# The two normalizations of tile 17 on VectorE, moved ahead of three of its other instructions

## The chip, the core and the metric

The kernel runs on one core of a Trainium2 chip. A core has TensorE (PE, matrix multiplications into the eight banks of PSUM), VectorE (DVE), ScalarE (ACT), GpSimd (POOL) and SyncE (SP, here only an issuer of DMAs), each with its own instruction queue that runs in order. The metric is the device time of one execution, in microseconds (us); of several runs the median is given.

## What is computed

Two layers, one behind the other, for 4 sequences of 768 tokens. The first is a retention layer with 8 heads of 64 channels. In the form of a recurrence, for each batch and head with its decay gamma:

```python
state = gamma * state + outer(k[t], v[t])
y[t] = (1 / sqrt(D)) * q[t] @ state
```

The heads' y side by side are the 512 channels of x. The second layer normalizes and applies two matrices with a relu between them, and adds x:

```python
xn = (x - mean(x)) / sqrt(var(x) + 1e-6) * g_ln
out = x + relu(xn @ w_ch1) @ w_ch2          # 512 -> 2048 -> 512
```

## The kernel before

The 3072 tokens are cut into 24 tiles of 128: tiles 0 to 3 are the first of each sequence, 4 to 8 the other five of sequence 0, 9 to 13 those of sequence 1, 14 to 18 of sequence 2, 19 to 23 of sequence 3. In each tile the recurrence is written as a masked product of scores within the tile plus a product of q with the state of the tiles before.

The whole program is one long list of tokens (ORDER, lines 36 to 96). Each token calls a small function that issues a few instructions. Nothing reorders them: every engine runs its instructions in the order in which the tokens stand, and the framework adds the semaphore waits between the engines, for data, for buffers that are used again, and also where two engines read the same PSUM bank one after the other. A number behind the letters is the tile (or group), "a" and "b" are the even and the odd heads, "/A" or "/S" is an engine, and what stands behind "//" names PSUM banks. The tokens that matter here:

- k, q, v (GpSimd, L337): loads of a tile. gk, gq, gv (GpSimd, L366): one element copied out of a buffer that is to be loaded again, which makes GpSimd's queue wait until the buffer is free.
- tr (SP, L380): one DMA that transposes q and k of a tile. eq (VectorE, L386): the transposed q times a table of scales, 128x512, both inputs bf16 in SBUF.
- vg (GpSimd, L457): v times a table of decays, 128x512, both inputs in SBUF.
- pd (TensorE, L465): adds a tile's contribution to the state in bank PD. pb (VectorE, L475, two instructions): writes a scaled copy of it, the state for the next tile.
- vis (TensorE, L395 and L401): the "visit" of a pair of tiles. Scores of the first tile (8 matmuls), of the second (8), then 16 matmuls L401 of q with the state, which open banks Y0 and Y1 anew. Y0 takes the even heads of both tiles, Y1 the odd ones.
- am (VectorE, L408): scores times the mask. py (TensorE, L423): these times v, on top of Y.
- bn (VectorE, L431 and L432): mean and variance of y. xn (VectorE, L441): (y - mean) times g_ln, from bank Y to SBUF. xc (ScalarE, L447): a plain copy of y from bank Y to SBUF, for the sum at the end. sq (ScalarE, L508): the square roots of a group's variances; rs (VectorE, L513) the reciprocals.
- ex (SP, L495): the transposition of xn by DMA. m (TensorE, L520): a group's product with w_ch1, in banks X0 to X3. r (L531 on ScalarE): the relu of it, to SBUF.
- z (TensorE, L543): a tile's product with w_ch2 in four parts. ad (VectorE, L550): that times 1/deviation plus x. st (ScalarE's queue, L557): the store.

The tiles are processed in pairs from tile 8 on, and z of one tile, m and r of a group, and the visits are woven into each other, so that TensorE has work all the time. The pair of the change, 16 and 17, has its statistics behind it, and the next visit is that of tiles 18 and 19. On TensorE the order there is m10_14, z12_1, z12_2, z12_3, vis18, pd20, z13_0, z13_1, py18; on ScalarE r10_14, xc16b, sq11, xc16a, xc17a, xc17b; on GpSimd gv20, vg20, gq21, vg21, vg22, k23, v23; on SP tr21, ex17, ex16, tr22.

The three functions whose calls change places, or that stand next to them:

```python
    def _(eng, t):   # eq
        x = bank(("tp", "q", t), True) if t < T0 else slot(tr, t - T0)[:, 0:NPAIR, :]
        nc.vector.tensor_tensor(out=slot(trq, t), in0=x, in1=qsc, op=ALU.mult)
...
    def _(eng, t, half):   # xn
        dst, src, g = y_parts(t, half, slot(xns, t))
        nc.vector.scalar_tensor_tensor(out=dst, in0=src, scalar=mv[:, t, 0:1], in1=g,
                                       op0=ALU.subtract, op1=ALU.mult)
...
    def _(eng, t, half):   # xc
        dst, src, _ = y_parts(t, half, x_all[:, t, :])
        nc.scalar.copy(out=dst, in_=src)
```

Of the kernel before, what the change touches and what calls it, by code (L numbers as in the profile page):

```python
# [72 lines left out]
xc15a r10_6/A vis16//X0,X2,X3,X1 z10_3 am17a am17b m11_6//X3 ad10 gv18 v21 gv19 m11_8//X1  # L73
r11_8/A r11_6/A am16a am16b z11_0//M k21 gk20 vg19/ q21 v22 py16 m11_2//X1 r11_2/A py17 pd3
z11_1 bn16 pb19 m10_8//X1 m10_12//X2 xn16a bn17 gk21 m11_4//X3 z11_2 q22 k22 q23 r11_4/A r10_8/A
z11_3 gv20 r10_12/A m11_10//X1 vg20/ xn16b ad11 pd19 gq21 r11_10/A z12_0//M m10_14//X0 eq18 tr21
vg21/ pb20 xn17a eq19 xn17b vg22/ z12_1 r10_14/A xc16b z12_2 sq11 xc16a xc17a xc17b z12_3 k23
v23 vis18//X3,X0,X1,X2 ad12 ex17/S ex16/S tr22 pd20 am18b z13_0//M am18a z13_1 am19a py18 z13_2
bn18 z13_3 xn18b am19b m11_12//X0 py19 m11_0//X3 xn18a ad13 bn19 ex18/S m11_14//X2 st10/A
r11_0/A xn19b z14_0//M z14_1 r11_14/A xn19a eq21 st13/A xc19b r11_12/A xc18a xc18b z14_2 rs11  # L80
pb21 eq20 ex19/S sq12 xc19a z14_3 tr23 vis20//X1,X2,X0,X3 ad14 pd21 am21a z15_0//M z15_1 eq22
am20a am21b am20b z15_2 pb22 py21 py20 m12_1//X2 bn20 r12_1/A xn20b xn20a m12_4//X1 r12_4/A
# [565 lines left out]
```

## Time and profile before

| what | us |
|---|---|
| median of 3 runs | 212.17 (212.1 to 215.47) |
| the profiled execution, its own time | 212.35 |
| its span, first to last instruction | 210.5 |
| TensorE busy | 204.3 |
| VectorE busy | 127.7 |
| ScalarE busy | 76.9 |
| GpSimd busy | 96.5 |

The profile is of one execution. A row of a timeline gives the start in us from the beginning of the span, the length, the engine, the line of the kernel, the operation, the tile written and the tiles read (without their numbers, so that tile 18's rows are told from tile 19's by the written order), and the number of merged instructions; in brackets stands the idle time of the engine before it and what ended it. In the list of waits a row gives who waited for whom, the sum in us, how often, and the longest. PEld are TensorE's weight loads, which run beside its matmuls. The granted clock of TensorE was 1.000 for the whole span.

### The profile page before, as it was taken

Reading aid. Unit: us, or ns where it says so; the run is one execution under the profiler, and the core shown is the slowest. Engines: PE = TensorE matmul, PEld = TensorE weight load, DVE = VectorE, ACT = ScalarE, POOL = GpSimd, SP = SyncE. Lnnn points to the kernel's source line nnn. Section 1 sums busy time; section 2 is a strip of 40 time slices with the busy share of each in tenths; the row PEclk is TensorE's granted clock in tenths of the full one; section 3 lists DMA queues with packets and bytes.
Section 4 is the critical chain, followed back from the end, with each engine's and each line's share of the span. In section 5 each row is a group of like instructions: output and inputs, shape, how many; then the busy total and the mean of one; then the engine's idle time right before and its main releaser. Section 6 shows DMA issues by size and latency. Waiting matters only on the chain.

```text
span 210.5 us, 4985 instructions
## 1 busy us (share of the span) xinstructions
PE 204.3 (97%) x2031; PEld 131.8 (63%) x2031; DVE 127.7 (61%) x297; ACT 76.9 (37%) x168; POOL 96.5 (46%) x145
## 2 busy tenths in 40 slices
PE   7898999999999999999999999999999999999994
PEld 2467999897548667676587686475545444444443
DVE  4797889587248878578695566868948402110023
ACT  6265653642400334515237124314281522346000
POOL 8996593495597797780587449500000000000000
PEclk9999999999999999999999999999999999999999
DMA  9999999999999999999999999996032400015005
GB/s 127 172 181 180 163 195 167 125 172 161 159 121 190 123 178 138 150 118 188 225 145 172 170 166 110 137 108 149 1 104 100 101 0 3 0 50 201 0 3 199
DMA packets 109946, 27.11 MB, mean 129 GB/s; under 512 B 102625, under 2 KB 106977, under 8 KB 109922
## 3 DMA queue, kind: packets, MB, share of 16 engines
q0 software_dynamic: 77024, 13.37, 84.6%
q1 hardware_dynamic: 28242, 6.85, 24.0%
q10 hardware_dynamic: 4656, 6.56, 9.7%
q8 instruction: 16, 0.26, 0.5%
q14 instruction: 8, 0.07, 0.1%
HBM read 27.30 MB, written 6.29 MB: 160 GB/s over the span
## 4 chain that ended last, share of the span: by engine, by line
PE 89%; DVE 8%; ACT 1%; issue 1%; DVEq 0%; ACTq 0%
PE X L520 38%; PE M L543 25%; PE Y L543 9%; PE PD L543 4%; PE X L395 3%; PE Y L423 3%; PE PD L465 2%; PE PD L564 2%; DVE trq L386 2%; DVE asb L408 2%; DVE xn L441 1%; PE Y L401 1%; DVE mask L303 1%; PE Y L372 1%; DVE bns L431 1%
## 5 line engine op out<-in xcount | busy, mean ns | idle before, releaser
L520 PE MATMUL X<-xnt,w 128*128 128x128 bf16 (+2 forms) x896 | 93.9, 257 | 0.0
L531 ACT ACTIVATE h<-X 128x512 bf16<-128x512 f32 x89 | 51.2, 602 | 80.6 <-PE X L520 68.7
L520 PEld LDWEIGHTS <-w 128*128 128x128 bf16 x896 | 66.1, 98 | 20.5 <-issue 0.2
L543 PE MATMUL M<-w,h 128*128 128x512 bf16 x256 | 61.5, 379 | 0.0
L543 PEld LDWEIGHTS <-h 128*128 128x128 bf16 x400 | 37.3, 98 | 37.9
L408 DVE TENSOR_TENSOR asb<-X,mask 128x512 bf16<-128x512 f32 x48 | 30.6, 684 | 11.1 <-PE X L395 10.8
L457 POOL TENSOR_TENSOR vg<-v,vsc 128x512 bf16<-128x512 bf16 x20 | 21.3, 1069 | 9.7 <-DMA v<-in_v_dram 8.6
L550 DVE SCALAR_TENSOR_TENSOR osb<-M,rstd,x_all 128x512 f32<-128x512 f32 x16 | 11.9, 746 | 20.4 <-PE M L543 20.0
L447 ACT CAST x_all<-Y 128x256 bf16<-128x256 f32 (+1 forms) x39 | 14.3, 410 | 26.4 <-DVE xn L441 26.4
L337 POOL DMA_DIRECT2D v<-in_v_dram x24 | 21.8, 910 | 3.7 <-DMA w<-in_moe_w_ch_dram 2.5
L431 DVE BATCH_NORM_STATS2 bns<-Y 128x6 f32<-128x256 f32 (+1 forms) x39 | 16.3, 455 | 9.2 <-PE Y L423 9.0
L543 PE MATMUL Y<-w,h 128*128 128x512 bf16 (+1 forms) x96 | 21.8, 370 | 0.0
L441 DVE SCALAR_TENSOR_TENSOR xn<-Y,mv,gb 128x256 bf16<-128x256 f32 (+1 forms) x39 | 18.7, 513 | 1.2 <-PE Y L423 0.6
L475 DVE TENSOR_TENSOR state<-PD,gch 64x256 bf16<-64x256 f32 x40 | 16.6, 415 | 0.6 <-PE PD L465 0.3
L337 POOL DMA_DIRECT2D qk<-in_q_dram x17 | 15.2, 895 | 1.1 <-issue 1.1
L337 POOL DMA_DIRECT2D qk<-in_k_dram x17 | 15.3, 898 | 0.9 <-issue 0.7
L550 DVE SCALAR_TENSOR_TENSOR osb<-PD,rstd,x_all 128x512 f32<-128x512 f32 (+1 forms) x3 | 1.9, 618 | 20.1 <-PE PD L543 20.1
L386 DVE TENSOR_TENSOR trq<-tr,qsc 128x512 bf16<-128x512 bf16 x17 | 10.1, 597 | 3.6 <-DMA tr<-qk 3.4
L366 POOL COPY scrap<-qk 1x1 bf16<-1x1 bf16 x28 | 5.5, 195 | 11.5 <-DMA qk<-in_k_dram 9.7
L564 PE MATMUL PD<-zeros 128*128 128x512 bf16 (+1 forms) x33 | 9.0, 410 | 1.2 <-DVE zeros L250 1.2
L423 PEld LDWEIGHTS <-asb 128*128 128x128 bf16 x192 | 8.0, 98 | 3.5 <-DVE asb L408 1.6
L543 PE MATMUL PD<-w,h 128*128 128x512 bf16 (+1 forms) x48 | 8.8, 326 | 0.0
(75 smaller groups left out, 131.8 us busy)
## 6 DMA issues: line engine op xcount, KB each, us to landing
out_dram<-osb ACTq DMA_DIRECT2D x23, 256.0 KB, 2.4
w<-in_moe_w_ch_dram POOLq DMA_DIRECT2D x8, 512.0 KB, 9.2
v<-in_v_dram POOLq DMA_DIRECT2D x24, 128.0 KB, 6.6
qk<-in_k_dram POOLq DMA_DIRECT2D x17, 128.0 KB, 6.7
qk<-in_q_dram POOLq DMA_DIRECT2D x17, 128.0 KB, 5.5
k<-in_k_dram POOLq DMA_DIRECT2D x6, 128.0 KB, 8.2
q<-in_q_dram POOLq DMA_DIRECT2D x6, 128.0 KB, 7.8
tr<-qk SPq DMA_TRANSPOSE x17, 5.5
```

The costliest lines, as they stand in the source:

```text
L337: nc.gpsimd.dma_start(out=dst, in_=tok[kind][TILES[t]])
L386: nc.vector.tensor_tensor(out=slot(trq, t), in0=x, in1=qsc, op=ALU.mult)
L408: nc.vector.tensor_tensor(out=slot(asb, t)[:, :, par, :], in0=bank(("pa", t, par)).rearrange("p (i t) -> p i t", t=P), in1=mask.rearrange( ...
L423: nc.tensor.matmul(dst, lhsT=slot(asb, t)[:, h // 2, h % 2, :], rhs=v_of(t)[:, h, :], start=(not late and n == H and h == 0), stop=(h >= H ...
L431: nc.vector.bn_stats(out=bns[:, t, i, :], in_=x)
L441: nc.vector.scalar_tensor_tensor(out=dst, in0=src, scalar=mv[:, t, 0:1], in1=g, op0=ALU.subtract, op1=ALU.mult)
L447: nc.scalar.copy(out=dst, in_=src)
L457: nc.gpsimd.tensor_tensor(out=slot(vgs, chunk(t)), in0=v_of(t), in1=vsc[:, c, :].unsqueeze(2).to_broadcast([P, H, D]), op=ALU.mult)
L475: nc.vector.tensor_tensor(out=slot(state, chunk(t) - 1)[o, :, o], in0=pd[o, :, o], in1=gch[o, c - 1, :].unsqueeze(2).to_broadcast([D, NPAI ...
L520: nc.tensor.matmul(bank(("mm", g, ho))[:, j * n * P:(j + 1) * n * P], lhsT=w1[:, ko, (ho + j) * P:(ho + j + 1) * P], rhs=x[:, x0:x0 + n, k ...
L531: nc.scalar.activation(out=dst, in_=src, func=AF.Relu)
L543: nc.tensor.matmul(bank(("m2", t, piece))[:, 0:hi - lo], lhsT=slot(h1, t // 4)[:, ho, t % 4 * P:(t % 4 + 1) * P], rhs=w2[:, ho, lo:hi], st ...
```

## The change

Two tokens, xn17a and xn17b, which stood on both sides of eq19, are moved up by some tokens, to stand ahead of eq18. They pass eq18, tr21, vg21, pb20 and eq19; of these eq18, pb20 and eq19 are VectorE's. All other tokens keep their order; most of the lines of the diff are only wrapped anew.

```diff
 z11_3 gv20 r10_12/A m11_10//X1 vg20/ xn16b ad11 pd19 gq21 r11_10/A z12_0//M m10_14//X0 eq18 tr21
-vg21/ pb20 xn17a eq19 xn17b vg22/ z12_1 r10_14/A xc16b z12_2 sq11 xc16a xc17a xc17b z12_3 k23
-v23 vis18//X3,X0,X1,X2 ad12 ex17/S ex16/S tr22 pd20 am18b z13_0//M am18a z13_1 am19a py18 z13_2
...
+z11_3 gv20 r10_12/A m11_10//X1 vg20/ xn16b ad11 pd19 gq21 r11_10/A z12_0//M m10_14//X0 xn17a
+xn17b eq18 tr21 vg21/ pb20 eq19 vg22/ z12_1 r10_14/A xc16b z12_2 sq11 xc16a xc17a xc17b z12_3
+k23 v23 vis18//X3,X0,X1,X2 ad12 ex17/S ex16/S tr22 pd20 am18b z13_0//M am18a z13_1 am19a py18
...
```

More of the change, by code (lines that the diff above doesn't have):

```diff
@@ L75 @@
 z11_1 bn16 pb19 m10_8//X1 m10_12//X2 xn16a bn17 gk21 m11_4//X3 z11_2 q22 k22 q23 r11_4/A r10_8/A
-z11_3 gv20 r10_12/A m11_10//X1 vg20/ xn16b ad11 pd19 gq21 r11_10/A z12_0//M m10_14//X0 eq18 tr21
-vg21/ pb20 xn17a eq19 xn17b vg22/ z12_1 r10_14/A xc16b z12_2 sq11 xc16a xc17a xc17b z12_3 k23
-v23 vis18//X3,X0,X1,X2 ad12 ex17/S ex16/S tr22 pd20 am18b z13_0//M am18a z13_1 am19a py18 z13_2
-bn18 z13_3 xn18b am19b m11_12//X0 py19 m11_0//X3 xn18a ad13 bn19 ex18/S m11_14//X2 st10/A
+z11_3 gv20 r10_12/A m11_10//X1 vg20/ xn16b ad11 pd19 gq21 r11_10/A z12_0//M m10_14//X0 xn17a
+xn17b eq18 tr21 vg21/ pb20 eq19 vg22/ z12_1 r10_14/A xc16b z12_2 sq11 xc16a xc17a xc17b z12_3
+k23 v23 vis18//X3,X0,X1,X2 ad12 ex17/S ex16/S tr22 pd20 am18b z13_0//M am18a z13_1 am19a py18
+z13_2 bn18 z13_3 xn18b am19b m11_12//X0 py19 m11_0//X3 xn18a ad13 bn19 ex18/S m11_14//X2 st10/A
 r11_0/A xn19b z14_0//M z14_1 r11_14/A xn19a eq21 st13/A xc19b r11_12/A xc18a xc18b z14_2 rs11
```

## The prediction

> **What bounds the kernel now.** I read the page first: the busy shares, then the chain that ended last.
>
> ```profile
> span 210.5 us, 4985 instructions
> PE 204.3 (97%) x2031; PEld 131.8 (63%) x2031; DVE 127.7 (61%) x297; ACT 76.9 (37%) x168; POOL 96.5 (46%) x145
> PE 89%; DVE 8%; ACT 1%; issue 1%; DVEq 0%; ACTq 0%
> ```
>
> TensorE is nearly always busy and makes 89% of the chain. So a change of VectorE's order can win only where TensorE stands still, and can lose only by making it stand still. The list of waits for TensorE from 30 to 160 us has one entry:
>
> ```profile
> PE Y L401 <- ACT x_all L447: 0.3, 1, 0.3
> ```
>
> Next I looked for its place, in TensorE's timeline. These are the visits 18 and 20 (start, length, line). The second is the same stretch with nothing in its way.
>
> ```profile
> 133.79 0.62 PE L395 MATMUL X<-trq,tr 64*128 64x128 bf16 x16
> 134.72 0.67 PE L401 MATMUL Y<-state,trq 64*128 64x64 bf16 x16 [0.30 <-ACT x_all L447]
> 135.31 0.40 PE L465 MATMUL PD<-vg,qk 128*128 128x128 bf16 x4
> ...
> 145.64 0.62 PE L395 MATMUL X<-trq,tr 64*128 64x128 bf16 x16
> 146.09 0.40 PE L401 MATMUL Y<-state,trq 64*128 64x64 bf16 x16
> 146.42 0.40 PE L465 MATMUL PD<-vg,qk 128*128 128x128 bf16 x4
> ```
>
> From the first score matmul to pd there are 1.52 us in visit 18 (135.31 - 133.79) and 0.78 in visit 20 (146.42 - 145.64). The wait costs 0.74 us of TensorE's time; the 0.3 of the list is a part of it, since the weight loads stall too. It is the only such place, so 0.74 us is also the most that this change can win.
>
> Who makes it? ScalarE's copies of x (xc), then VectorE's xn17b, then eq19. ScalarE's and VectorE's timelines:
>
> ```profile
> 131.31 0.60 ACT L531 ACTIVATE h<-X 128x512 bf16<-128x512 f32 x1 [1.36 <-PE X L520]
> 133.56 0.37 ACT L447 CAST x_all<-Y 128x256 bf16<-128x256 f32 x1 [1.66 <-DVE xn L441]
> ...
> 128.47 0.75 DVE L550 SCALAR_TENSOR_TENSOR osb<-M,rstd,x_all 128x512 f32<-128x512 f32 x1 [1.96 <-PE M L543]
> 129.14 0.42 DVE L386 TENSOR_TENSOR trq<-tr,qsc 128x512 bf16<-128x512 bf16 x1
> 129.57 0.86 DVE L475 TENSOR_TENSOR state<-PD,gch 64x256 bf16<-64x256 f32 x2
> 130.46 0.49 DVE L441 SCALAR_TENSOR_TENSOR xn<-Y,mv,gb 128x256 bf16<-128x256 f32 x1
> 130.86 2.27 DVE L386 TENSOR_TENSOR trq<-tr,qsc 128x512 bf16<-128x512 bf16 x1
> 133.06 0.47 DVE L441 SCALAR_TENSOR_TENSOR xn<-Y,mv,gb 128x256 bf16<-128x256 f32 x1
> ```
>
> By the written order these six are ad11, eq18, pb20, xn17a, eq19, xn17b. All four xc stand behind xn17b, which ended at 133.53, and they ran from 133.56 to 134.94; the last two matmul waits end at 134.72 and 134.99. And xn17b was late because eq19 took 2.27 us where the median of its kind is 0.42. GpSimd's timeline gives the cause I take:
>
> ```profile
> 129.69 1.03 POOL L457 TENSOR_TENSOR vg<-v,vsc 128x512 bf16<-128x512 bf16 x1
> 130.68 0.18 POOL L366 COPY scrap<-qk 1x1 bf16<-1x1 bf16 x1
> 130.81 2.03 POOL L457 TENSOR_TENSOR vg<-v,vsc 128x512 bf16<-128x512 bf16 x2
> ```
>
> These are vg20, gq21, and vg21 with vg22. eq19 came 0.05 us after vg21 began and ended 0.29 us after vg22's end (133.13 against 132.84): held, then run. The xn beside vg20 (130.46, 0.49 us) was not held.
>
> **The change, part by part.** No instruction is added or removed. VectorE's order becomes ad11, xn17a, xn17b, eq18, pb20, eq19, ad12. The other engines keep their order.
>
> *xn17a and xn17b, earlier.* Their input is long there (bn17 ends at 126.17) and an xn follows another at 0.40 us elsewhere (pairs take 0.88). xn17a starts at 129.14 in eq18's old place, xn17b ends at 129.14 + 0.88 = 130.02. That is 3.51 us earlier than 133.53.
>
> *What waits for xn17b.* ScalarE has the relu r10_14 (131.31 to 131.91) ahead of the xc, so the four xc with sq11 start at about 131.9, not at 130.0. With the same 1.38 us (133.56 to 134.94) they end at 133.3. Undisturbed, TensorE wants to begin L401 at 133.79 + 0.45 = 134.24. The wait is gone, with 0.9 us to spare. SP's two transposes ex17 and ex16 go out at about 130.1 instead of 133.59, tr22 behind them goes earlier if its loads have landed, and st10 on ScalarE's queue (133.58 before) goes some 2 us earlier. None is near an end: group 12 reads those transposes at 149.71, and eq21 and eq22, which need tr21 and tr22, stand at 143.40 and 147.01 with no idle time before them. I cost the earlier DMA traffic at nothing; that slack of over 6 us covers it.
>
> *eq18, later.* It used to end at 129.56, before vg20. Now it comes at about 129.95, inside vg20 (129.69 to 130.72). It is held; the question is until when. The nearest rows:
>
> ```profile
> 73.85 1.06 POOL L457 TENSOR_TENSOR vg<-v,vsc 128x512 bf16<-128x512 bf16 x1
> 74.84 0.40 POOL L366 COPY scrap<-qk 1x1 bf16<-1x1 bf16 x1
> 73.92 1.28 DVE L386 TENSOR_TENSOR trq<-tr,qsc 128x512 bf16<-128x512 bf16 x1
> ```
>
> There, an eq waits for one vg followed by a gate copy, just as vg20 is followed by gq21. It ended at 75.20, 0.29 us after the vg, and the copy behind was stretched from 0.18 to 0.40. So the eq gets in before the copy. That is the low end: eq18 ends at 130.72 + 0.29 = 131.0, gq21 at about 131.05. The high end comes from eq19's own row, where an eq stayed out over the end of a vg into the next: eq18 then ends at 133.13. I take the low end, since vg and then copy is exactly the order here.
>
> *pb20 and eq19.* pb20 (0.86) runs from 131.0 to 131.85; its input is there from 129.5. eq19 follows at 131.85, inside vg21, which the held copy has moved to about 131.0 to 132.05. With vg22 straight behind, eq19's old row says it waits for both: vg22 ends at 133.05, eq19 at 133.35. At the other end it gets in between and ends at 132.35. Both are before 133.79, when TensorE ends z12_3 and comes to visit 18, so the two ends cost the same: nothing. GpSimd's k23 and v23 go out about 0.25 us later, with eq23 at 151.85.
>
> In the Trainium skill, the page "SBUF — State Buffer", section "Who interferes with whom", says that a VectorE instruction with two SBUF inputs and a GpSimd instruction that reads SBUF block each other fully, the later one until the first finishes. This rule speaks against the change, which moves eq18 from ahead of vg20 to a place inside it; the trace agrees on the hold (2.27 us against 0.42) but eq19 stayed out past the instruction that was first, which the section doesn't foresee. By the section alone eq18 ends at 131.0 and eq19 at about 132.3; by the 2.27 us row for both they end at 133.1 and 134.4; the sum is -0.74 by the one and about -0.3 by the other.
>
> *What is late next.* With pd at 134.57, z13_0 wants bank M at 134.81. ad12 frees it at 134.65 (133.90 + 0.75, it waits for z12_3 and not for the change); ScalarE's release of L401 took 0.05 us, so some 0.1 us is left. py18 moves to 136.54 and needs am18a (135.85). bn18 has 1.31 us of idle time ahead, of which 0.74 goes. Behind it TensorE is busy without a break to 207.6, so the gain stays.
>
> **Sum.** -0.74 us on TensorE's path, 0 for the rest: span 210.5 to 209.8, and that execution's own 212.35 to 211.6. The median shown is 0.18 below that execution, which would give 211.4. I predict 211.5.
>
> **Rivals.**
>
> *B: eq18 is held to the end of vg22.* For it: eq19's 2.27 us row. Against it: the row at 73.92. eq18 ends at 133.13, pb20 at 133.95, eq19 at 134.37. Visit 18 starts with tile 18 and stands before tile 19 until about 134.43; the rest (0.23 of scores, 0.33 of L401) puts pd at 134.99, where 135.31 was. Gain 0.32: 211.9.
>
> *C: slower.* One mechanism: B's hold, with GpSimd's chain of vg later against TensorE. Place: the wait of tile 19's score matmuls for eq19. It decides from eq19's end at 134.70 on, that is with vg22 ending after 133.17 instead of 132.84; every 0.1 us beyond costs 0.1. GpSimd waits for loads shortly before (2.87 us for qk, to 126.49), so a shift of 1 us is possible. eq19 then ends at 135.4, pd starts at 136.0: +0.7, or 212.9. Against it: the first hold must be long, too.
>
> *D: nothing changes,* because ScalarE's copies wait for something else or L401 does. Then 212.2. Against it: ScalarE's row names xn, and its start follows xn17b's end by 0.03 us.
>
> **How the numbers follow.** Chances: forecast 0.62, B 0.18, D 0.07, C 0.13. The forecast's own range is 211.2 to 211.8 (the offset of 0.18 to the median either way, and 0.1 for ad12). The range goes from 211.1 to 212.9, which takes in B, D and most of C. 2% is 4.2 us, about what a measurement of this kernel can tell from no change, and no case here reaches it. For a mechanism that I have not seen I leave 0.02 below and 0.05 above: one of the runs before was at 215.47, so this kernel can lose more than the parts above explain.
>
> **What would show it.** Right: both xn between 129.1 and 130.1; the xc at about 131.9; no wait at L401, and 0.78 us from the first score matmul to pd; eq18 at about 1.05 us, a gate copy of 0.4, eq19 at about 1.5. Wrong: eq18 over 2 us (B), TensorE waiting at L395 for trq (B or C), the xc still ending close to L401's start (D), or a new wait of z13_0 for ad12.

## The result, and the profile after

The changed kernel takes 211.13 us (median of 21 runs, 210.53 to 214.24), the kernel before, run beside it, 212.76 (21 runs, 211.12 to 215.47). The ratio is 0.994 with a 95% interval of 0.9913 to 0.9967: a gain of 1.27 us, somewhere between 0.70 and 1.85. The ratio compares the means without the few slow runs (211.32 and 212.59), so it says less than the 1.63 us between the medians. The 211.13 us lie within the range, 0.03 above its lower end, and the gain is small, as forecast. But the traces show that the path to it was not the one that was forecast.

The page of the changed kernel, first the span and the engines' busy time:

```profile
span 209.7 us, 4961 instructions
PE 202.2 (96%) x2007; PEld 131.6 (63%) x2031; DVE 127.7 (61%) x297; ACT 76.7 (37%) x168; POOL 95.4 (45%) x145
```

The work is the same (the few matmuls missing on TensorE are missing from the record, since its weight loads are as many as before). The span is 0.8 us shorter. The list of TensorE's waits, from 30 to 160 us, no longer holds the one entry of before; it has three others:

```profile
PE M L543 <- issue: 0.5, 3, 0.2
PE X L395 <- DVE trq L386: 0.3, 1, 0.3
PE M L543 <- DVE osb L550: 0.2, 1, 0.2
```

L401 waits for ScalarE's copies no more. In its place L395 waits for trq, which is what eq writes; the waits at L543 lie between 75 and 118 us, ahead of the change. TensorE's timeline shows where, at visit 18:

```profile
133.16 0.40 PE L395 MATMUL X<-trq,tr 64*128 64x128 bf16 x8
133.84 0.40 PE L395 MATMUL X<-trq,tr 64*128 64x128 bf16 x8 [0.28 <-DVE trq L386]
134.06 0.41 PE L401 MATMUL Y<-state,trq 64*128 64x64 bf16 x16
134.41 0.40 PE L465 MATMUL PD<-vg,qk 128*128 128x128 bf16 x4
```

The eight score matmuls of tile 18 run, those of tile 19 stand 0.28 us, and L401 follows at once. From the first score matmul to pd there are 1.25 us (134.41 - 133.16). Before it was 1.52, undisturbed it is 0.78. So the change wins 0.27 us here, and leaves 0.47. VectorE's timeline:

```profile
127.85 0.75 DVE L550 SCALAR_TENSOR_TENSOR osb<-M,rstd,x_all 128x512 f32<-128x512 f32 x1 [1.96 <-PE M L543]
128.51 0.87 DVE L441 SCALAR_TENSOR_TENSOR xn<-Y,mv,gb 128x256 bf16<-128x256 f32 x2
129.30 3.26 DVE L386 TENSOR_TENSOR trq<-tr,qsc 128x512 bf16<-128x512 bf16 x1
132.48 0.85 DVE L475 TENSOR_TENSOR state<-PD,gch 64x256 bf16<-64x256 f32 x2
133.36 0.43 DVE L386 TENSOR_TENSOR trq<-tr,qsc 128x512 bf16<-128x512 bf16 x1
```

And GpSimd's and ScalarE's:

```profile
129.11 1.03 POOL L457 TENSOR_TENSOR vg<-v,vsc 128x512 bf16<-128x512 bf16 x1
130.10 0.18 POOL L366 COPY scrap<-qk 1x1 bf16<-1x1 bf16 x1
130.24 2.03 POOL L457 TENSOR_TENSOR vg<-v,vsc 128x512 bf16<-128x512 bf16 x2
...
131.17 0.37 ACT L447 CAST x_all<-Y 128x256 bf16<-128x256 f32 x1
131.62 0.92 ACT L447 CAST x_all<-Y 128x256 bf16<-128x256 f32 x3
```

The xn pair is done at 129.38 and the copies at 132.54, well ahead of L401, as forecast. But eq18 took 3.26 us: it stood from 129.30 behind vg20, the gate copy, vg21 and vg22, and ended at 132.56, 0.29 us after the last of them (132.27). pb20 and eq19 came behind it, and eq19 ended at 133.79. TensorE wanted it at about 133.4. This is rival B.

The rest of the 0.8 us has nothing to do with visit 18: it began at 133.16 instead of 133.79, 0.63 us earlier. The shift was there ahead of the change: ad11, VectorE's last instruction before it, came at 127.85 instead of 128.47, and TensorE had started visit 8 at 61.83 instead of 62.83. So in single profiles positions ahead of the change scatter by more than it wins. Behind it nothing is given back: from pd20 to the first score matmul of visit 20 there are 10.32 us, and 10.33 before.

### The profile page after: what moved, and what is told of

Same layout as the page of the kernel before. It is cut to its first block, busy times and chain, and to the rows that moved or that the text cites. A ratio compares the mean times of both kernels' runs of the same rounds, so it can differ in the third digit from the quotient of the medians.

```text
span 209.7 us, 4961 instructions
## 1 busy us (share of the span) xinstructions
PE 202.2 (96%) x2007; PEld 131.6 (63%) x2031; DVE 127.7 (61%) x297; ACT 76.7 (37%) x168; POOL 95.4 (45%) x145
## 4 chain that ended last, share of the span: by engine, by line
PE 54%; DVE 4%; issue 1%
PE X L520 23%; PE M L543 16%; PE Y L543 6%; PE PD L543 4%; DVE trq L386 2%; PE X L395 2%; PE Y L423 1%; PE PD L465 1%; DVE state L475 1%; PE Y L401 1%; DVE osb L550 1%; DVE xn L441 0%; DVE rstd L513 0%
## 5 line engine op out<-in xcount | busy, mean ns | idle before, releaser
L543 PEld LDWEIGHTS <-h 128*128 128x128 bf16 x400 | 37.4, 98 | 38.2 <-issue 0.3
L543 PE MATMUL M<-w,h 128*128 128x512 bf16 x238 | 59.4, 379 | 1.5 <-issue 0.5
L543 PE MATMUL Y<-w,h 128*128 128x512 bf16 (+1 forms) x93 | 21.7, 370 | 0.2
L386 DVE TENSOR_TENSOR trq<-tr,qsc 128x512 bf16<-128x512 bf16 x17 | 10.8, 643 | 3.5 <-DMA tr<-qk 3.3
L564 PE MATMUL PD<-zeros 128*128 128x512 bf16 (+1 forms) x32 | 8.5, 402 | 1.2 <-DVE zeros L250 1.2
L366 POOL COPY scrap<-qk 1x1 bf16<-1x1 bf16 x28 | 4.9, 176 | 9.8 <-DMA qk<-in_k_dram 8.5
L543 PE MATMUL PD<-w,h 128*128 128x512 bf16 (+1 forms) x46 | 8.4, 324 | 0.1
```

The costliest lines, as they stand in the source:

```text
L543: nc.tensor.matmul(bank(("m2", t, piece))[:, 0:hi - lo], lhsT=slot(h1, t // 4)[:, ho, t % 4 * P:(t % 4 + 1) * P], rhs=w2[:, ho, lo:hi], st ...
```

## The experiments

A correction first. The gate copies of GpSimd were described above as waiting for a buffer to be free. In the trace they wait for a load to land, such as that of k21 for 2.87 us, to 126.49. GpSimd's timeline of the kernel before:

```profile
126.49 0.18 POOL L366 COPY scrap<-qk 1x1 bf16<-1x1 bf16 x1 [2.87 <-DMA qk<-in_k_dram]
```

The chain of vg follows from there at GpSimd's own pace: vg20 starts 3.19 to 3.28 us after this copy in all nine profiles of the table further down. This matters below.

The diffs are cut to the tokens of one engine, in that engine's order; the other engines' tokens that stand between them are left out. "Stretch" is the time on TensorE from visit 18's first score matmul to pd20: 0.78 if nothing waits. T1 and T2 differ on where the 1.27 us come from, T3 on what sets the gain, T4 and T5 on when a held eq gets in.

### e1 and e2: both kernels once more

No edit.

> The kernel before, once more, against itself. Two theories stand. T1: the change wins only at visit 18 of TensorE (0.27 us in the two profiles, 1.52 against 1.25 us from the first score matmul to pd), and the rest of the 1.2 us between the medians is spread between executions that arises ahead of the change. T2: the whole 1.2 us comes from the change, because in most executions TensorE stands longer at L401 in the kernel before than in the one execution that was profiled. T1 expects a ratio of 1.000 with an interval of some 0.003 either way, a stretch in visit 18 of about 1.5 us (1.4 to 1.7), and the start of visit 18 up to 1 us away from 133.8. T2 expects the same ratio, but a stretch well above 1.5, near 2.5.

> The changed kernel, once more, on the chip of the others. T1 expects a ratio of about 0.9987 (0.27 of 212 us) with 0.997 to 1.000 possible, eq18 held again for about 3 us until GpSimd's last vg has ended, and a stretch of 1.2 to 1.3 us in visit 18. T2 expects a ratio near 0.994.

The kernel before against itself: 0.9989 (0.9949 to 1.0029), stretch 1.54 (135.64 - 134.10). The changed kernel: 0.995 (0.9914 to 0.9986), stretch 1.04 (136.38 - 135.34), with eq18 held for 3.06 us. So the stretches fall as T1 says: neither profile of the kernel before comes near the 2.5 us of T2. The ratio is again nearer to T2's. With intervals of 0.3 to 0.4% to either side this run alone hardly rules out T1's 0.9987 (its upper end is 0.9986). What is in VectorE's order must decide, so the next runs change that.

### e3: eq18 back in front

```diff
-xn17a xn17b eq18 pb20 eq19
+eq18 xn17a xn17b pb20 eq19
```

> eq18 goes back to its old place ahead of the two xn; pb20 and eq19 stay behind them. T1 expects eq18 to take 0.42 us (it ends before vg20 starts), eq19 to be held by vg21 and vg22 for about 1.6 to 2 us and to end 0.3 us after vg22, before TensorE reaches visit 18, and so no wait in visit 18: a stretch of 0.78 us, 0.74 below the kernel before (ratio 0.9965) and 0.47 below the changed one. If the hold is not from the vg but from the place in the order, eq18 or the instruction behind the xn is long here, too. T2 expects a ratio of 0.992 or less, below that of the changed kernel by another 0.5 us.

The expectation failed, and the run is the most useful one. The ratio was 0.996 (0.9924 to 0.9996), but eq18, in front, was held all the same. VectorE's and GpSimd's timelines:

```profile
127.97 0.75 DVE L550 SCALAR_TENSOR_TENSOR osb<-M,rstd,x_all 128x512 f32<-128x512 f32 x1 [1.96 <-PE M L543]
128.64 3.02 DVE L386 TENSOR_TENSOR trq<-tr,qsc 128x512 bf16<-128x512 bf16 x1
...
128.22 1.03 POOL L457 TENSOR_TENSOR vg<-v,vsc 128x512 bf16<-128x512 bf16 x1
129.35 2.03 POOL L457 TENSOR_TENSOR vg<-v,vsc 128x512 bf16<-128x512 bf16 x2
```

In this execution vg20 began 0.25 us after ad11 (128.22 against 127.97), where it was 1.22 in the profile before and 1.26 in the one after. So eq18, which comes 0.67 us after ad11, found vg20 running. The stretch was 1.01. The place of GpSimd's chain against VectorE's changes from one execution to the next, and it isn't set by the order on VectorE. That became T3.

### e4 and e7: vg21 and vg22 out of the way

The same edit on GpSimd, in e4 with the changed order of VectorE, in e7 with the old one:

```diff
-vg20 gq21 vg21 vg22 k23 v23
+vg20 gq21 k23 v23 vg21 vg22
```

> The changed kernel with vg21 and vg22 moved on GpSimd behind the loads k23 and v23, so that eq18 meets vg20 and a gate copy alone and eq19 meets no vg. If the vg hold eq18 (T1), eq18 takes about 1.1 to 1.4 us instead of 3.26, eq19 0.42, visit 18 has a stretch of 0.78 us, and the ratio is 0.9965 (0.74 us). If something else holds it (the DMA of the transposes, the bank of Y), eq18 stays near 3 us and the ratio is that of the changed kernel. T2 expects 0.992 or less in the first case.

> The order of the kernel before on VectorE, with vg21 and vg22 moved on GpSimd behind the loads k23 and v23. If eq19's 2.27 us come from these two vg, eq19 takes 0.43 to 0.9 us here, xn17b ends at about 131.6 to 132, the copies xc are done before TensorE comes to visit 18, and the stretch there is 0.78 us with VectorE's order unchanged: the whole of what the change could win (0.74 us in the profile, a ratio of 0.996 to 0.9965). If the copies are late for another reason, the stretch stays near 1.5 and the ratio at 1.000.

e4: eq18 took 1.39 us, the stretch was 0.78, the ratio 0.9957 (0.9921 to 0.9994). VectorE's and GpSimd's timelines:

```profile
130.24 1.39 DVE L386 TENSOR_TENSOR trq<-tr,qsc 128x512 bf16<-128x512 bf16 x1
...
129.59 1.03 POOL L457 TENSOR_TENSOR vg<-v,vsc 128x512 bf16<-128x512 bf16 x1
130.58 0.18 POOL L366 COPY scrap<-qk 1x1 bf16<-1x1 bf16 x1
130.70 0.94 POOL L337 DMA_DIRECT2D qk<-in_k_dram  x1
```

Here vg20 came 0.80 us after ad11, so the stretch alone doesn't show what the vg are worth; eq18's 1.39 us against 3.26 does. e7, VectorE's timeline with the order of before, and the three rows of visit 18 on TensorE:

```profile
131.17 0.84 DVE L386 TENSOR_TENSOR trq<-tr,qsc 128x512 bf16<-128x512 bf16 x1
131.93 0.47 DVE L441 SCALAR_TENSOR_TENSOR xn<-Y,mv,gb 128x256 bf16<-128x256 f32 x1
134.21 0.75 DVE L550 SCALAR_TENSOR_TENSOR osb<-M,rstd,x_all 128x512 f32<-128x512 f32 x1 [1.80 <-PE M L543]
...
134.10 0.62 PE L395 MATMUL X<-trq,tr 64*128 64x128 bf16 x16
134.56 0.40 PE L401 MATMUL Y<-state,trq 64*128 64x64 bf16 x16
134.89 0.40 PE L465 MATMUL PD<-vg,qk 128*128 128x128 bf16 x4
```

eq19 takes 0.84 us instead of 2.27, xn17b ends at 132.40, the stretch is 0.79, with vg20 as late (1.17 us after ad11) as in the kernel before. So it was the two vg that made eq19 long, and eq19 that made the copies late. The whole of what can be won at visit 18 is won without touching VectorE. The time says less than the trace: 0.9981 (0.9945 to 1.0017).

### e8: eq19 ahead of pb20

```diff
-xn17a xn17b eq18 pb20 eq19
+xn17a xn17b eq18 eq19 pb20
```

> The changed kernel with eq19 ahead of pb20. The changed kernel's stretch of 1.25 us is, by the reading of its profile, made of eq18's hold and of pb20 (0.85 us) standing between eq18 and eq19. Then eq19 ends 0.85 us earlier here, before or just at TensorE's coming to visit 18, and the stretch is 0.78 to 0.85 us, 0.4 to 0.47 below the changed kernel; the ratio to the kernel before is 0.996 to 0.9965. If TensorE waits at tile 19 for another reason, the stretch stays at 1.25.

Stretch 0.79 (135.70 - 134.91), ratio 0.9972 (0.9935 to 1.0009). Held together with eq18 (3.09 us for both), eq19 is done 0.8 us ahead of visit 18, and pb20, which nobody waits for yet, comes behind it. The stretch alone doesn't show what this order is worth, since vg20 came 0.75 us after ad11 here and 1.26 in the profile of the changed kernel: with pb20 in between, eq19 would have ended at about 135.0 here, still before TensorE wants it at 135.14. But in the changed kernel's profile eq19 ended 1.23 us after eq18 (133.79 against 132.56). Without pb20's 0.85 us it would have ended at about 132.9, ahead of visit 18 at 133.16. By this estimate, what the changed kernel still lost was eq18's hold plus pb20 in front of eq19.

### e5 and e6: GpSimd's chain early on purpose

The load q23 is moved behind vg22, in e5 with the old order of VectorE and in e6 with the changed one:

```diff
-q22 k22 q23 gv20 vg20 gq21 vg21 vg22 k23
+q22 k22 gv20 vg20 gq21 vg21 vg22 q23 k23
```

> The order of the kernel before on VectorE, with GpSimd's load q23 moved behind vg22, so that vg20, gq21, vg21 and vg22 come about 0.87 us earlier against VectorE. In one execution (eq18 first) GpSimd was that early by itself, and eq18, although it was the first of the six, was held for 3.0 us. T3: how much the change is worth depends on where GpSimd's chain of vg lies when eq18 comes. If it lies behind eq18, as in the profile before, the change wins 0.3 us; if vg20 starts ahead of eq18, the old order loses more, since all six then stand behind the hold and the copies xc stand behind the sixth. T3 expects here eq18 held for about 3 us, xn17b ending at about 134.3 instead of 133.5, the copies at 135.7, and a stretch from visit 18's first score matmul to pd of about 2.3 us, against 1.52 with GpSimd late: 0.4% slower than the kernel before (ratio 1.002 to 1.004). T1 (the gain is a fixed 0.3) expects a stretch near 1.5 and a ratio of 1.000.

> The changed order with the same early chain of vg. T3 expects eq18 held for some 2.3 us, eq19 done at about 133.5, TensorE at visit 18 without a wait or with one of 0.2 us at most, a stretch of 0.78 to 1.0 us, and so 1.3 to 1.5 us less than the old order with the early chain (ratio to the kernel before 0.996 to 0.997, to the old order with the early chain 0.993). T1 expects 0.3 us less than the old order with the early chain.

TensorE's timeline of e5, then of e6:

```profile
134.09 0.62 PE L395 MATMUL X<-trq,tr 64*128 64x128 bf16 x16
135.64 0.66 PE L401 MATMUL Y<-state,trq 64*128 64x64 bf16 x16 [0.93 <-ACT x_all L447]
136.23 0.40 PE L465 MATMUL PD<-vg,qk 128*128 128x128 bf16 x4
```

```profile
135.34 0.62 PE L395 MATMUL X<-trq,tr 64*128 64x128 bf16 x16
135.80 0.40 PE L401 MATMUL Y<-state,trq 64*128 64x64 bf16 x16
136.12 0.40 PE L465 MATMUL PD<-vg,qk 128*128 128x128 bf16 x4
```

With vg20 0.22 us after ad11, the old order has a stretch of 2.14 us: eq18 is held (3.00 us), pb20, xn17a, eq19 and xn17b stand behind the hold, and the copies stand behind xn17b. The changed order with the early chain has 0.78. Here the change is worth 1.36 us in the traces, as T3 says, not a fixed 0.3. The ratios to the kernel before are 1.0014 (0.9989 to 1.004) and 0.9974 (0.9939 to 1.0009), some 0.85 us apart, with intervals that overlap. In e6 the chain lay still earlier than in e5 (vg20 0.30 us ahead of ad11), so the two are not at the same offset; by e5's offset eq18 would end 0.5 us later, still in time for a stretch of about 0.8 (an estimate).

### e11: the kernel before, for its offset

No edit.

> The kernel before, one more look, for where GpSimd's chain of vg lies against VectorE when nothing is changed. T3 expects vg20 to start 0.2 to 1.3 us after ad11; if over 0.67, eq18 is free, eq19 held and the stretch in visit 18 is about 1.5 us; if under, eq18 is held for about 3 us and the stretch is about 2.1 us.

vg20 started 1.09 us after ad11, eq18 was free, eq19 took 2.15 us, the stretch was 1.40 (134.73 - 133.33). As T3 expects for a late chain.

The nine profiles of kernels in which GpSimd's part up to vg20 is untouched:

| kernel | vg20 after ad11, us | stretch, us |
|---|---|---|
| before | 1.22 | 1.52 |
| e1, before | 1.23 | 1.54 |
| e11, before | 1.09 | 1.40 |
| after | 1.26 | 1.25 |
| e2, after | 1.07 | 1.04 |
| e3, eq18 first | 0.25 | 1.01 |
| e4, changed, vg later | 0.80 | 0.78 |
| e7, old order, vg later | 1.17 | 0.79 |
| e8, eq19 ahead of pb20 | 0.75 | 0.79 |

At a like offset (1.2 or 1.1) the change is worth 0.27 to 0.36 us. In both kernels the stretch falls along with the offset, since the chain's end comes earlier against TensorE, until the offset falls under 0.67; there the old order loses its free eq18 and goes up to 2.14, and the changed one does not (e5 and e6). One profile of nine was under 0.67.

### e9 and e10: what stands ahead of vg20

On GpSimd, q23 moves between gv20 and vg20; e10 also has vg21 and vg22 behind the loads. VectorE has the changed order.

```diff
-q23 gv20 vg20 gq21 vg21 vg22 k23 v23
+gv20 q23 vg20 gq21 vg21 vg22 k23 v23      (e9)
+gv20 q23 vg20 gq21 k23 v23 vg21 vg22      (e10)
```

> The changed order on VectorE; on GpSimd the load q23 stands between gv20 and vg20 instead of ahead of gv20. The step of the prediction that failed said that eq18 gets in after vg20, ahead of the gate copy, as an eq did at 73.92 us; there a load's issue stood ahead of the vg, while ahead of vg20 stands a gate copy. T4: what stands ahead of the vg decides. Then eq18 ends 0.29 us after vg20 here (1.0 to 1.3 us long), gq21 is stretched to 0.4, and eq19 is held by vg21 and vg22 and ends about 1 us ahead of where eq19 ends in the changed kernel, for a stretch of 0.78 us in visit 18. T5: what follows the copy decides (a vg or a load, against a second copy at 73.92). Then eq18 is held for about 3 us as in the changed kernel, and the stretch is 1.2 to 1.3 us.

> The same with vg21 and vg22 behind k23 and v23, so that vg20 and gq21 stand alone between two loads. With a gate copy ahead of vg20, eq18 ended 0.87 us after the end of gq21. T4 expects eq18 to end 0.29 us after vg20 and gq21 to be stretched to 0.4 us. T5 expects eq18 to end about 0.87 us after gq21 again. The stretch in visit 18 is 0.78 us by both.

The two rows of e10 and, below, those of e9 (VectorE, then GpSimd):

```profile
129.66 0.85 DVE L386 TENSOR_TENSOR trq<-tr,qsc 128x512 bf16<-128x512 bf16 x1
129.16 1.06 POOL L457 TENSOR_TENSOR vg<-v,vsc 128x512 bf16<-128x512 bf16 x1
130.15 0.40 POOL L366 COPY scrap<-qk 1x1 bf16<-1x1 bf16 x1
```

```profile
130.01 2.31 DVE L386 TENSOR_TENSOR trq<-tr,qsc 128x512 bf16<-128x512 bf16 x1
129.88 1.05 POOL L457 TENSOR_TENSOR vg<-v,vsc 128x512 bf16<-128x512 bf16 x1
130.87 0.18 POOL L366 COPY scrap<-qk 1x1 bf16<-1x1 bf16 x1
131.00 2.21 POOL L457 TENSOR_TENSOR vg<-v,vsc 128x512 bf16<-128x512 bf16 x2
```

e10 is what T4 expects: eq18 ends at 130.51, 0.29 us after vg20, and the copy is stretched to 0.40, where with a gate copy ahead of vg20 (e4) it got in only behind the copy. e9 is what neither expects: eq18 doesn't get in before the copy but ends at 132.32, and the two vg take 2.21 instead of 2.03, so it got in between vg21 and vg22. Other rows of these traces point the way of T4: in five profiles (before, e3, e7, e10, e11) an eq came into the vg at about 73 us, which stands behind a load's issue, and each time it ended 0.29 us behind that vg; in six (after, e2, e3, e4, e5, e8) an eq came into vg20 behind a gate copy, and none got in there. So what stands ahead of the vg seems to have a part in it, but e9 shows that it does not decide alone. A rule for when a held eq gets in can't be read from these runs and stays open. Both stretches were 0.78. e9, e10 and e11 were timed once each (211.68, 211.34 and 211.76 us, the kernel before 212.18), too little to compare.

## Why the prediction was right, and where it was not

**The bound and its place: right.** TensorE's only listed wait from 30 to 160 us was at L401 of visit 18, made by the copies behind xn17b behind eq19 behind vg21 and vg22. e7 shows each link: with the two vg gone, eq19, xn17b and the copies come early and the stretch is 0.79.

**The xn and the copies: right.** The pair took 0.87 us (0.88 forecast), ScalarE's copies followed the relu, and L401 lost its wait. The earlier transposes and stores cost nothing on TensorE's path, where 10.32 us follow pd20 as before.

**eq18: wrong, and this is the step that failed.** "I take the low end, since vg and then copy is exactly the order here." It was the high end: eq18 ended at vg22's end plus 0.29. One row like the case in two instructions was taken for the case; the row differed in what stood ahead of them (a load's issue there, a gate copy here). With the load there eq18 did get in ahead of the copy in e10, but not in e9, so why it was the high end stays open.

**pb20 and eq19: wrong as a consequence.** They were put at nothing and were not hidden: eq19 ended at 133.79, 0.4 us after TensorE wanted it. Rival B's working held: its stretch was 1.20 (134.99 - 133.79), measured 1.25 and 1.04. So the change gave 0.27 to 0.36 us of the 0.74 in the profiles with a late chain.

**"The most that this change can win" is 0.74: wrong.** This took one execution's offset for the kernel's. In e5, with GpSimd's chain early, the old order has 1.36 us over the minimum of 0.78.

**The page of the Trainium skill.** "SBUF — State Buffer", section "Who interferes with whom", has the later one wait until the first finishes. Every hold beside a vg here agrees that it waits; after its first vg, eq18 waited for three more instructions of GpSimd in the changed kernel (3.26 us) and for none in e10.

**The total: within the range, in part by luck, and not fully explained.** The forecast took 0.67 us off the median shown before (212.17 to 211.5), and the gain measured over 21 runs each is 0.70 to 1.85. But the traces give less: 0.3 us in eight profiles of nine and 1.36 in the ninth make an estimated mean of 0.42 us, from the table and e5 and e6. So the forecast came near with a step that failed, and 211.13 is below its own 211.2 to 211.8 and below B's 211.9. e2's runs say 0.30 to 1.83. The kernels whose stretch is at its minimum should win more than the changed kernel, and their ratios are 0.9957, 0.9974, 0.9981 and 0.9972 (e4, e6, e7, e8), against 0.994 and 0.995. So the timings don't order these kernels as the traces do; their intervals of 0.25 to 0.4% to either side are as wide as what is to be told apart. Whether the remaining 0.3 us and more are chance, or more executions with an early chain than one in nine (an estimate: about four in ten would be needed for 0.70), or something else, was not shown. Rival C (a longer hold with a late chain) did not come up: no offset in the table exceeds the 1.22 of the kernel before by more than 0.04.

## What to carry to other kernels

When an instruction's time in the profile is five times its median, look at what runs beside it on an engine that can hold it up, and count the wait through the whole unbroken chain there, not to the end of the first instruction. Two engines whose queues are paced by different things (here loads that land, and TensorE) slide against each other between executions; a gain read from one profile at one offset should be worked out at the other side of the slide as well. And a chain on one engine is best ordered by who is waited for first: pb20 went last in e8 without a wait on TensorE.

## What the runs showed of the hardware

Behind a gate copy that is followed by a load's issue, an eq ended 0.87 us (e4: 131.63 against 130.76) and 0.88 us (e7: 132.01 against 131.13) after the one-element copy's recorded end, not 0.29 as behind a vg. So GpSimd kept it out for some 0.6 us after its copy seemed done, in the time of the issue. Whether the copy or the issue did so was not separated by these two. But in e3 an eq came at 109.65, 0.62 us after a gate copy's end and in the middle of a load's issue (109.31 to 110.26), with no vg beside it until 110.40; it took 1.11 us and ended 0.50 us after the issue. So a load's issue seems able to hold an eq by itself. It does not always: eq18 in the kernel before came 0.47 us into the issue of q23 (128.67 to 129.57) and took 0.42.

The other way round, an eq that got in held GpSimd: the gate copy of 0.18 us took 0.40 in e10, and the two vg 2.21 instead of 2.03 in e9.
